# A decode block on one core: three edits around loads and the last softmax

## Chip, cores and metric

The kernel runs on one core of a Trainium2 chip. The metric is device microseconds (us) of one execution. All arithmetic is in 32-bit floats, and the core has a matrix engine (PE), a vector engine (DVE), a scalar engine (ACT), GpSimd (POOL) and a sync engine (SP). SP and ACT issue the transfers, which run on the core's 16 DMA engines.

## The reference

One token for each of four sequences goes through a layernorm, attention over the last 1024 positions of a cache (16 query heads, 8 key heads, head size 256), an output projection with a residual, and then an MLP with two layernorms before it.

```python
x = A_x                                            # (4, 1, 448)
h = x + attention(layernorm(x), k_cache, v_cache, wq, wo)
#   q = x @ wq; p = softmax(q k^T / 16) over the last 1024 keys; (p v) @ wo
h2 = h + mlp(layernorm(h))
#   y = layernorm(.); gelu(y @ w1 + b1) @ w2 + b2,  w1 (448, 1792), w2 (1792, 448)
```

## The kernel before, in words

All that is read from memory, about 88 MB, passes once through three large buffers ("slots", the tiles `t0`, `ta`, `tb`, `tc`, `td`, `te`). A slot of some 8 MB is filled by one or a few loads, used, and refilled when the products that read it are done. The host packs caches and weights so that each slot holds what a stage needs: `ta` has keys, query weights and the first half of the values of a head, `tb` the other half, output weights and the next keys, and so on.

SP issues all of these loads, in the order of the code: `wq0` with the transposed x (L262), `k0`, the keys of head 0 (L265), two small pieces of query weights `wq1_last` (L267), then `ta`, `tb`, `tc`, `td` twice (L290 to L311, all issued by the helper at L57), then the last slots `te`: keys of head 7, values and output weights of heads 6 and 7 (`vo`), `w1` in two loads and `w2` in three of 8, 4 and 2 chunks (L321 to L328). A chunk of w2 is 128 x 448 numbers. ACT issues four small transfers of 11 KB, the rows of x and of both biases (L127), into the tile `rs`, which is read only behind the attention.

Each transfer reports its end on one of eight counters, DMAHW0 to DMAHW7. The framework deals them in turn to the transfers in the order in which it schedules them, over SP's and ACT's queues together. A transfer that gets a counter for the second time first waits, on the engine that issues it, until the earlier user of that counter has landed. SP takes its instructions strictly in order, so what stands behind a waiting load waits too. In the kernel before, the order is `wq0` (0), `k0` (1), four rows (2 to 5), two `wq1_last` (6, 7), and then `ta` gets 0 again, `tb` 1, `tc` 2.

PE's order is that of the code. For a head it does the scores `s` (L174), DVE takes the maximum `mx` (L179), ACT the exponential `p` (L190), PE transposes it into `ppt` (L206), DVE copies that into `pT` (L210), and PE multiplies by the values into `po` (L218). Around the last softmax, where no other work is ready, the kernel issues products of a zero tile, `idle`, that nobody reads (L336): two between the scores of head 7 and the transposes, and ten between the transposes and the values of head 6 (L338 to L342). Then come head 6's output, head 7's values, the residual, the layernorms, and the MLP: `pu` from w1 (L416), `pa` from the first eight chunks of w2 (L449), `py` from the last six (L459), and the write of `out`.

Of the kernel before, what the change touches and what calls it, by code (L numbers as in the profile page):

```python
# [15 lines left out]
B, D = 4, 448  # L16
# [4 lines left out]
P = 128  # L21
# [3 lines left out]
NFC = F // P  # L25
FQ = F // 4
Q = 32
CACHE = NKC * B * DH
# [7 lines left out]
def block_kernel(ctx: ExitStack, tc, rows, wq0, k0, wq1, la, lb, lc, ld, k7, vo, w1, w2, out):  # L36
    nc = tc.nc
# [12 lines left out]
    def slot(name):  # L50
        return ring.tile([P, SLOT], F32, tag="r", name=name)

    def load(t, at, src, pieces=None):
        dst = t[:, at : at + src.shape[-1]]
        at = 0
        for n in pieces or (src.shape[-1],):
            nc.sync.dma_start(dst[:, at : at + n], src[:, at : at + n])  # L57
            at += n
        return dst

    def cut(t, sizes):
        parts, at = [], 0
        for n in sizes:
            parts.append(t[:, at : at + n])
            at += n
        return parts
# [11 lines left out]
    def keys(t):  # L78
        return t.rearrange("p (c b k) -> p c b k", c=2, b=B)
# [22 lines left out]
    yT = const.tile([P, ND + 1, Q], F32, name="yT")  # L102
# [21 lines left out]
    rs = const.tile([P, 2 * P + FQ], F32, name="rs")  # L124
    nc.gpsimd.memset(rs, 0.0)
    for j in range(4):
        nc.scalar.dma_start(rs[j * Q : j * Q + B, :], rows[j])  # L127
    xb, b2b, b1b = rs[:, :P], rs[:, P : 2 * P], rs[:, 2 * P :]


# [39 lines left out]
    def scores_half(g, h, kt):  # L170
        s = ps_s.tile([P, 512], F32, tag="s", name=f"s{g}_{h}")
        for c in range(2):
            for b in range(B):
                nc.tensor.matmul(  # L174
                    s[b * Q : (b + 1) * Q, :], qT[g % 2][:, c, b, :], kt[:, c, b, :],
                    start=(c == 0), stop=(c == 1),
                )
        m = work.tile([P, 1], F32, tag=f"mx{h}", name=f"mx{g}_{h}")
        nc.vector.reduce_max(m, s, axis=AX.X)  # L179
        return s, m  # L180

    def softmax(g, parts):
        halves, mx = zip(*parts)
        nm = work.tile([P, 1], F32, tag="nm", name=f"nm{g}")
        nc.vector.tensor_max(nm, mx[0], mx[1])
        nc.vector.tensor_scalar_mul(nm, nm, -SCALE)  # L186
        p = once.tile([P, 2 * 512], F32, tag="p", name=f"p{g}")
        sums = work.tile([P, 2], F32, tag="sums", name=f"sums{g}")
        for h in range(2):
            nc.scalar.activation(  # L190
                p[:, h * 512 : (h + 1) * 512], halves[h], AF.Exp, bias=nm, scale=SCALE,
                accum_out=sums[:, h : h + 1],
            )
        rec = work.tile([P, 1], F32, tag=f"rec{g % 3}", name=f"rec{g}")
        nc.vector.tensor_add(rec, sums[:, 0:1], sums[:, 1:2])
        nc.vector.reciprocal(rec, rec)
        return p, rec

    def scores(g, kt):
        return softmax(g, [scores_half(g, h, kt[h]) for h in range(2)])  # L200

    def transpose_p(g, p):
        for h in range(2):
            pt = ps_t.tile([P, 4, P], F32, tag="t", name=f"ppt{g}_{h}")
            for c in range(4):
                nc.tensor.transpose(pt[:, c, :], p[:, (4 * h + c) * P : (4 * h + c + 1) * P], ident)  # L206

            src = pt.rearrange("p (c i) (b q) -> p c i b q", i=2, b=B)
            for i in range(2):
                nc.vector.tensor_copy(  # L210
                    pT[g % 2][:, 2 * h : 2 * h + 2, :, i * REP : (i + 1) * REP], src[:, :, i, :, :REP]
                )
# [44 lines left out]
    def po_tile(g, pool=ps_o, tag="o"):  # L257
        return pool.tile([P, 2, DH], F32, tag=tag, name=f"po{g}")
# [22 lines left out]
    p, rec = scores(0, [keys(ka), keys(kb)])  # L281
# [7 lines left out]
    for g in (0, 3):  # L289
        ka, kb, wqt, va = cut(load(slot(f"ta{g}"), 0, la[g // 3]), (HALF, HALF, WEIGHTS, HALF))  # L290
        p, rec_next = scores(g + 1, [keys(ka), keys(kb)])
# [8 lines left out]
        p, rec_then = scores(g + 2, [keys(ka), keys(kb)])  # L300
# [11 lines left out]
        p, rec = softmax(g + 3, [first_half, scores_half(g + 3, 1, keys(kb))])  # L312
# [7 lines left out]
    g = HKV - 2  # L320
    e = [slot(f"te{i}") for i in range(3)]  # L321
    kt = [keys(t) for t in cut(load(e[0], 0, k7), (HALF, HALF))]
# [2 lines left out]
    vt_last = chunks(load(e[2], 0, vo[1][:, :CACHE], (CACHE // 4, CACHE // 2, CACHE // 4)))  # L325
    wo_last = output_weights(load(e[1], CACHE + WEIGHTS, vo[1][:, CACHE:]))
    w1t = cut(load(e[0], CACHE, w1, (2 * F, F + F // 2)), (F, F, F, F // 2))
    w2t = cut(load(e[2], CACHE, w2, (8 * D, 4 * D, 2 * D)), NFC * (D,))  # L328
    p, rec_last = scores(g + 1, kt)


    warm0 = ps_o.tile([P, 512], F32, tag="o", name="warm0")

    def keep_warm(n, warm):
        for _ in range(n):
            nc.tensor.matmul(warm[:Q], idle[:, :Q], idle, start=True, stop=True)  # L336

    keep_warm(2, warm0)  # L338
    transpose_p(g + 1, p)
    keep_warm(10, warm0)  # L340
    po = po_tile(g)
    values(g, vt, po)  # L342
    po_last = po_tile(g + 1, ps_t, "t")
# [17 lines left out]
    for i in range(4):  # L361
        for j in range(4):
            nc.tensor.matmul(
                ph[j * Q : (j + 1) * Q], oT[(g + 1) % 2][:, i, :], columns(wo_last[:, i, :], j),
                start=False, stop=(i == 3),
# [3 lines left out]
    def w1_part(a, j):  # L369
        if a < 3:  # L370
            return slice(0, P), w1t[a][:, FQ * j : FQ * (j + 1)]
        rows = slice(H * (j // 2), H * (j // 2) + H)
        return rows, w1t[a][rows, FQ * (j % 2) : FQ * (j % 2 + 1)]
# [38 lines left out]
    for a in range(ND):  # L412
        m = Q if a == 0 else B
        for j in range(4):
            rows, w = w1_part(a, j)
# [31 lines left out]
    for c in range(first):  # L447
        j, m = c % 4, Q if c < 4 else B
# [6 lines left out]
    for c in range(first, NFC):  # L455
        for j in range(4):
            m, n = (Q, 2) if c == first else (B, 2 if j < 3 else 1)
# [80 lines left out]
```

## Time and profile before

| | us |
|---|---|
| median of three runs | 215.27 |
| lowest and highest | 214.98, 215.72 |
| the profiled execution, its own time | 214.81 |
| its span, first to last instruction | 213.0 |

The profile is of one execution. Engine rows give busy time and what ended the idle time before it; "SPq" is SP's queue of issues; the chain of waits follows the last instruction back through whatever released each step.

### The profile page before, as it was taken

To read this page: it belongs to the slowest core of one execution; us is meant where nothing else is said; L and a number is where in the kernel's file an instruction comes from. 1 tells how busy PE (TensorE), PEld (TensorE's weight loads), DVE (VectorE), ACT (ScalarE), POOL (GpSimd) and SP (SyncE) were. 2 spreads that over 40 slices of the span, in tenths; PEclk is the share of its full clock that TensorE was granted. 3 is DMA by queue.
4 is the path that set the end of the run, shared out by engine and by line. 5 is a ranking of instruction groups with operands and counts; after the bars stand their busy time and mean duration, and the time that the engine had idled before them with its cause. 6 is when DMAs were issued, how large, how long until landed. Compare 5 with 4: busy or idle time off the path is not lost.

```text
span 213.0 us, 2294 instructions
## 1 busy us (share of the span) xinstructions
PE 137.4 (64%) x971; PEld 48.2 (23%) x971; DVE 38.4 (18%) x167; ACT 21.2 (10%) x52; POOL 5.6 (3%) x17
## 2 busy tenths in 40 slices
PE   0456824872970595289398198239809876998993
PEld 0322211220220221023123022113202322334432
DVE  1420320320230012012114013100301223122320
ACT  0210110120020100021003001000000302000310
POOL 6100000000000000000000000000000000000110
PEclk9999995796697579769859959955965999999999
DMA  7999899999999999999999999999999998999990
GB/s 291 433 392 502 381 486 391 447 467 409 417 453 444 417 417 477 390 465 391 458 423 444 425 456 417 429 417 465 405 410 415 430 450 380 435 414 435 420 376 34
DMA packets 3289, 88.46 MB, mean 415 GB/s; under 512 B 384, under 2 KB 512, under 8 KB 1104
## 3 DMA queue, kind: packets, MB, share of 16 engines
q1 hardware_dynamic: 3248, 88.29, 96.7%
q8 instruction: 7, 0.11, 0.2%
q10 hardware_dynamic: 32, 0.05, 0.1%
q14 instruction: 2, 0.02, 0.0%
HBM read 88.26 MB, written 0.07 MB: 415 GB/s over the span
## 4 chain that ended last, share of the span: by engine, by line
DMA 64%; PE 29%; DVE 3%; ACT 1%; issue 1%; SPq 0%; ACTq 0%; DVEq 0%
DMA ta<-la 21%; DMA td<-ld 20%; DMA tb<-lb 16%; PE s L174 8%; DMA t<-k 8%; PE po L218 8%; PE ppt L206 2%; PE pu L416 2%; PE warm L336 1%; PE acc L247 1%; PE pq L154 1%; PE pot L239 1%; PE pa L449 1%; DVE o L235 1%; DVE mx L179 1%
## 5 line engine op out<-in xcount | busy, mean ns | idle before, releaser
L179 DVE TENSOR_REDUCE mx<-s 128x1 f32<-128x512 f32 x16 | 11.1, 691 | 61.0 <-PE s L174 61.0
L174 PE MATMUL s<-ta,qT 128*32 128x512 f32 x64 | 12.2, 935 | 8.9 <-DMA ta<-la 8.9
L156 ACT COPY qs<-pq 128x512 f32<-128x512 f32 x8 | 4.7, 585 | 112.3 <-PE pq L154 112.3
L190 ACT ACTIVATE p<-s,nm 128x512 f32<-128x512 f32 x16 | 10.9, 687 | 45.9 <-DVE nm L186 45.9
L174 PE MATMUL s<-td,qT 128*32 128x512 f32 x32 | 7.3, 1061 | 12.0 <-DMA td<-ld 12.0
L235 DVE TENSOR_SCALAR o<-po,rec 128x512 f32<-128x512 f32 x8 | 6.0, 751 | 47.1 <-PE po L218 47.1
L218 PE MATMUL po<-tb,pT 128*32 128x512 f32 x32 | 7.3, 1061 | 10.4 <-DMA tb<-lb 10.4
L154 PE MATMUL pq<-tc,yT 128*32 128x512 f32 (+1 forms) x20 | 3.9, 890 | 14.8 <-DMA tc<-lc 14.8
L206 PE MATMUL ppt<-ident,p 128*128 128x128 f32 x64 | 10.5, 286 | 2.0 <-ACT p L190 1.7
L218 PE MATMUL po<-tc,pT 128*32 128x512 f32 x64 | 10.5, 815 | 0.0
L160 PE MATMUL pqt<-ident,qs 128*128 128x128 f32 x32 | 6.6, 341 | 6.0 <-ACT qs L156 6.0
L174 PE MATMUL s<-tb,qT 128*32 128x512 f32 x64 | 9.1, 717 | 0.0
L206 PEld LDWEIGHTS ppt<-ident,p 128*128 128x128 f32 x64 | 6.7, 140 | 7.1 <-ACT p L190 7.1
L218 PE MATMUL po<-te,pT 128*32 128x512 f32 x64 | 7.9, 596 | 0.1
L162 DVE TENSOR_REDUCE sm<-pqt 128x16 f32<-128x64 f32 x8 | 1.8, 224 | 33.9 <-PE pqt L160 33.9
L174 PE MATMUL s<-t,qT 128*32 128x512 f32 x32 | 6.1, 925 | 2.6 <-DMA t<-k 2.6
L218 PE MATMUL po<-td,pT 128*32 128x512 f32 x64 | 7.3, 595 | 0.0
L336 PE MATMUL warm<-idle 128*32 128x512 bf16 x25 | 7.3, 382 | 0.0
L160 PEld LDWEIGHTS pqt<-ident,qs 128*128 128x128 f32 x32 | 4.2, 169 | 12.1 <-ACT qs L156 10.3
L174 PEld LDWEIGHTS s<-ta,qT 128*32 128x32 f32 x64 | 2.9, 163 | 17.4 <-issue 14.4
L239 PE MATMUL pot<-ident,o 128*128 128x128 f32 x32 | 5.2, 287 | 2.2 <-DVE o L235 2.2
L148 POOL TENSOR_TENSOR r<-ve_r,mhalf 128x1 f32<-128x1 f32 x2 | 1.1, 542 | 192.2 <-DVE ve_r L147 192.2
(129 smaller groups left out, 113.4 us busy)
## 6 DMA issues: line engine op xcount, KB each, us to landing
tc<-lc SPq DMA_DIRECT2D x2, 7936.0 KB
td<-ld SPq DMA_DIRECT2D x2, 7936.0 KB
ta<-la SPq DMA_DIRECT2D x2, 7040.0 KB, 29.4
tb<-lb SPq DMA_DIRECT2D x2, 7040.0 KB, 34.3
te<-vo SPq DMA_DIRECT2D x1, 4992.0 KB, 27.2
t<-k SPq DMA_DIRECT2D x1, 4864.0 KB, 16.4
te<-k SPq DMA_DIRECT2D x1, 4096.0 KB, 36.9
te<-w SPq DMA_DIRECT2D x2, 1792.0 KB, 28.0
```

What stands on the lines that cost most here:

```text
L154: nc.tensor.matmul(pq[j * Q : (j + 1) * Q, cols], y, w, start=True, stop=True)
L156: nc.scalar.copy(qs, pq)
L160: nc.tensor.transpose(pt[:, i, :], qs[:, i * P : (i + 1) * P], ident)
L174: nc.tensor.matmul(s[b * Q : (b + 1) * Q, :], qT[g % 2][:, c, b, :], kt[:, c, b, :], start=(c == 0), stop=(c == 1),)
L179: nc.vector.reduce_max(m, s, axis=AX.X)
L190: nc.scalar.activation(p[:, h * 512 : (h + 1) * 512], halves[h], AF.Exp, bias=nm, scale=SCALE, accum_out=sums[:, h : h + 1],)
L206: nc.tensor.transpose(pt[:, c, :], p[:, (4 * h + c) * P : (4 * h + c + 1) * P], ident)
L218: nc.tensor.matmul(po[b * Q : (b + 1) * Q], pT[g % 2][:, c, b, :], vt[c][:, :, b, :], start=(c == 0), stop=(c == NKC // 2 - 1),)
L235: nc.vector.tensor_scalar_mul(o, po, rec)
L239: nc.tensor.transpose(pt[:, i, c], o[:, i, c * P : (c + 1) * P], ident)
L336: nc.tensor.matmul(warm[:Q], idle[:, :Q], idle, start=True, stop=True)
L416: nc.tensor.matmul(pu[j * Q : j * Q + m, :], zT[rows, a, :m], w, start=(a == 0), stop=(a == ND - 1),)
```

## The change

There are three edits.

The rows of x and the biases go in seven transfers instead of four: for three of the four quarters the columns of x and b2 (256) and those of b1 (448) are separate transfers. ACT issues them.

The loads of `w2` are cut into 8, 3, 2 and 1 chunks instead of 8, 4 and 2.

Around the last softmax a new helper, `fill`, multiplies a part of the keys of head 7, which have landed, by `yT`, in 32-bit floats, into the same tile that nobody reads. Two such products take the place of the two of `idle` ahead of the transposes; behind the transposes one such product and two of `idle` stand where ten of `idle` stood.

```diff
@@ rows of x and biases
     for j in range(4):
-        nc.scalar.dma_start(rs[j * Q : j * Q + B, :], rows[j])
+        parts = (slice(0, 2 * P), slice(2 * P, 2 * P + FQ)) if j < 3 else (slice(0, 2 * P + FQ),)
+        for cols in parts:
+            nc.scalar.dma_start(rs[j * Q : j * Q + B, cols], rows[j][:, cols])
@@ loads of the second MLP weights
-    w2t = cut(load(e[2], CACHE, w2, (8 * D, 4 * D, 2 * D)), NFC * (D,))
+    w2t = cut(load(e[2], CACHE, w2, (8 * D, 3 * D, 2 * D, D)), NFC * (D,))
@@ around the last softmax
+    def fill(n):
+        for _ in range(n):
+            nc.tensor.matmul(warm0[:Q], yT[:, 0, :], kt[0][:, 0, 0, :], start=True, stop=True)
+
+    fill(2)
+    transpose_p(g + 1, p)
+    fill(1)
     keep_warm(2, warm0)
-    transpose_p(g + 1, p)
-    keep_warm(10, warm0)
     po = po_tile(g)
```

The seven transfers use up eight counters sooner, and the dealing shifts by three. SP's queue at the start of the program stood like this (a row is line, operation, destination and source, size, and the counters it waits for):

```order
L57 DMA t_134<-wq 128x1808
L57 DMA t_134<-k 128x9728
L267 DMA wq_last<-wq 32x1x512 x2
L57 DMA ta_239<-la 128x14080 [waits DMAHW0_49]
L57 DMA tb_313<-lb 128x14080 [waits DMAHW1_49]
```

SP's queue at the same place stands now like this:

```order
L57 DMA t_137<-wq 128x1808
L57 DMA t_137<-k 128x9728
L269 DMA wq_last<-wq 32x1x512 [waits DMAHW1_49]
L269 DMA wq_last<-wq 32x1x512 [waits DMAHW2_49]
L57 DMA ta_242<-la 128x14080 [waits DMAHW3_49]
L57 DMA tb_316<-lb 128x14080 [waits DMAHW4_49]
```

The wait for counter 1, which is that of `k0`, has moved from `tb` up to the first `wq_last`, two places ahead of `ta`; `ta` and `tb` now wait for rows (counters 3 and 4).

At the program's end SP's queue held the second load of w1, the loads of w2 and the write of the output with these waits (counters 0, 1 and 2 are there those of the keys of head 7, of head 6's values and of the first quarter of head 7's values):

```order
L57 DMA te_813<-w 128x2688
L57 DMA te_815<-w 128x3584 [waits DMAHW0_49]
L57 DMA te_815<-w 128x1792 [waits DMAHW1_49]
L57 DMA te_815<-w 128x896 [waits DMAHW2_49]
L466 DMA out<-res 128x128 [waits DMAHW3_49,DVE_49]
```

Now SP's queue ends with these:

```order
L57 DMA te_818<-w 128x3584 [waits DMAHW3_49]
L57 DMA te_818<-w 128x1344 [waits DMAHW4_49]
L57 DMA te_818<-w 128x896 [waits DMAHW5_49]
L57 DMA te_818<-w 128x448 [waits DMAHW6_49]
L473 DMA out<-res 128x128 [waits DMAHW7_49,DVE_49]
```

The first three wait for the same three landings as before, by their new counters; the added last load waits for the middle half of head 7's values (counter 6), and the output for their last quarter.

On PE, between the scores of head 7 and the values of head 6, the rows after the change are these (`idle` is the zero tile; the second name behind the arrow is the weights' side):

```order
L176 MATMUL s_1_842<-te_816,qT_112 32x512 x8
L342 MATMUL warm_863<-te_816,yT 32x512 x2
L208 MATMUL ppt_0_866<-ident,p_856 128x128 x4
L208 MATMUL ppt_1_873<-ident,p_856 128x128 x4
L342 MATMUL warm_863<-te_816,yT 32x512
L338 LDWEIGHTS idle
L338 MATMUL warm_863<-idle 32x512
L338 LDWEIGHTS idle
L338 MATMUL warm_863<-idle 32x512
L220 MATMUL po_883<-te_817,pT_113 32x512 x16
```

Ahead of the transposes two products of `idle` have become two of the keys, and behind them ten of `idle` have become one of the keys and two of `idle`; everything else on PE keeps its place.

## The prediction, as put on record

> **What bounds the kernel now.** I read the page's slices first, then the chain of waits, then the stretches by DMA, then SP's queue, since the change touches loads. The head of the page, its DMA rows and the chain by engine:
>
> ```profile
> span 213.0 us, 2294 instructions
> ...
> DMA  7999899999999999999999999999999998999990
> GB/s 291 433 392 502 381 486 391 447 467 409 417 453 444 417 417 477 390 465 391 458 423 444 425 456 417 429 417 465 405 410 415 430 450 380 435 414 435 420 376 34
> ...
> DMA 64%; PE 29%; DVE 3%; ACT 1%; issue 1%; SPq 0%; ACTq 0%; DVEq 0%
> ```
>
> The DMA engines are 90% busy or nearly so in every slice but the first and the last, and 64% of the chain is waiting for loads. The chain's long pieces (start, length):
>
> ```profile
> 1.18 16.36 DMA t<-k
> ...
> 17.56 34.27 DMA tb<-lb
> ...
> 61.75 44.26 DMA ta<-la
> ...
> 117.86 42.28 DMA td<-ld
> ...
> 160.19 3.64 PE s L174 x16
> ```
>
> Behind 160.19 no piece of the chain is a load: from there PE, DVE and ACT lead to the end. So two things end close together, the stream of loads and the chain of arithmetic behind the landing of `td`. How full the stream is shows in a stretch from the first large load to the end (busy times, granted clock, DMA share, GB/s) and at its last two microseconds:
>
> ```profile
> 5.40:207.00 201.60, 134.62 (x907) 46.76 (x911) 37.32 (x161) 20.67 (x51) 2.11 (x3) 0.84 1.00 429
> ...
> 208.00:209.00 1.00, 0.77 (x29) 0.48 (x24) 0.00 (x0) 0.53 (x1) 0.00 (x0) 1.00 0.11 43
> 209.00:210.00 1.00, 0.99 (x39) 0.68 (x28) 0.00 (x0) 0.00 (x0) 0.00 (x0) 1.00 0.00 0
> ```
>
> A share of 1.00 over 201.6 us means that there is no hole in which a late load could catch up. Microseconds in which the DMA engines have nothing to do are added to the time. That decides which of the three edits matters.
>
> **Seven transfers of rows.** The bytes are the same. ACT issues three more, but has nothing else until the first copy of q; the tile is read behind the attention. What counts is the dealing of the counters, since it changes what SP waits for. SP's queue at the start, and what it waited for:
>
> ```profile
> 0.73 0.39 SPq L57 DMA_DIRECT2D t<-wq  x1
> 1.18 0.41 SPq L57 DMA_DIRECT2D t<-k  x1
> 1.63 1.55 SPq L267 DMA_DIRECT2D wq_last<-wq  x2
> 5.36 0.34 SPq L57 DMA_DIRECT2D ta<-la  x1
> 17.56 0.33 SPq L57 DMA_DIRECT2D tb<-lb  x1
> ```
>
> ```profile
> SPq L57 <- DMA t<-k: 11.9, 1, 11.9
> SPq L57 <- DMA t<-wq: 2.2, 1, 2.2
> ```
>
> Before, `ta` waits for counter 0 (`wq0`, landed at 5.36) and `tb` for counter 1: it goes out at 17.56, when `k0` has landed, 11.9 us after SP came to it. This wait was free, because `ta` had been queued behind `k0` for 12 us and filled the engines. By the order of SP's queue the wait for counter 1 now stands at the first `wq_last`. So `wq_last` (two), `ta`, `tb` and all behind them stay in SP until `k0` lands. Then nothing at all is queued.
>
> The hole, step by step. `k0` lands at 17.54 as before, since it runs ahead of `ta` either way. Both `wq_last` are then issued, 1.55 us by the row above, and `ta` goes out at 17.56 + 1.55 = 19.11. `tb` follows at once, as its rows have long landed. When `ta` lands is worked out from these rows (size, us from issue to landing):
>
> ```profile
> ta<-la SPq DMA_DIRECT2D x1, 7040.0 KB, 29.4
> ...
> t<-wq SPq DMA_DIRECT2D x1, 904.0 KB, 4.6
> ```
>
> Before, `ta` landed at 5.36 + 29.4 = 34.76, 17.22 us behind `k0`; with the two pieces of 64 KB between them that is 7168 KB in 17.22 us, 416 KB/us. At that rate `ta` alone takes 16.9 us. A load into an idle queue also has a start and an end that nothing covers. No row shows this for 7 MB. Nearest is `wq0`: 4.6 us less 904/416 = 2.2 gives 2.4. Smaller is the write of `out`, 64 KB (issue, and what waited for its landing):
>
> ```profile
> 210.39 0.35 SPq L466 DMA_DIRECT2D out<-res  x1
> ```
>
> ```profile
> SPq L532 <- DMA out<-res: 1.2, 1, 1.2
> ```
>
> 0.35 + 1.2 less 64/416 = 0.15 gives 1.4. So `ta` lands at 19.11 + 16.9 + 1.4 to 2.4, that is 37.4 to 38.4, or 2.7 to 3.7 us later than before. I take 3.4, nearer to `wq0`, which is a load and starts from idle. The ends are wider. If `k0`, alone in the queue, lands half a microsecond sooner, the low end is 2.2. If the 128 KB of `wq_last` must pass ahead of `ta`, another 0.3 makes the high end 4.0.
>
> The Trainium skill, DMA: Bandwidth & Descriptors, section Anatomy of one DMA, gives a fixed cost of about 2.0 us per transfer beside bytes over 436 GB/s, fitted on GpSimd's path, where these are SP's. It speaks against making one load wait for another's landing. By it the hole would be 3.3 us and the sum below 217.5; by `wq0` it is 3.7 and 217.9; by `out` 2.7 and 216.9. The rows stand in the sum.
>
> The late `wq_last` itself is covered. It is issued at 17.6 and 18.4 and, at 1.5 to 2.4 us from there, lands by 21; its product comes behind 32 records of scores:
>
> ```profile
> L154 PE MATMUL pq<-wq_last,yT x2: 589/601/613, 24.5 to 25.0; 64*32 64x512 f32 x2
> ```
>
> It is needed at 24.5, with over 3 us to spare.
>
> **The products around the softmax.** PE in the timeline (start, length; in brackets the idle time before):
>
> ```profile
> 174.62 3.62 PE L174 MATMUL s<-te,qT 128*32 128x512 f32 x32
> ...
> 180.32 1.32 PE L206 MATMUL ppt<-ident,p 128*128 128x128 f32 x8 [1.68 <-ACT p L190]
> ...
> 181.57 2.33 PE L336 MATMUL warm<-idle 128*32 128x512 bf16 x10
> 181.68 0.26 DVE L210 COPY pT<-ppt 128x16 f32<-128x16 f32 x2 [0.23 <-PE ppt L206]
> ...
> 183.97 4.50 PE L218 MATMUL po<-te,pT 128*32 128x512 f32 x40
> ```
>
> A product of `idle` costs 2.33/10 = 0.23 us. A product of the keys has the shape of the scores: 16 of them, 32 records, take 3.62 us. They go to four column groups in turn, so if the groups work side by side one alone takes 0.9 us, if not 0.23. I take 0.9, since the new ones all go to one group. Two in front take 1.8 us from about 178.2, to 180.0, and fit into the idle 1.68 us: the transposes wait for `p` until 180.32 as before. If each took 0.2 more, the transposes would start 0.1 late. Behind the transposes stand now 0.9 + 2 x 0.23 = 1.36 us instead of 2.33, so the values of head 6 start 0.95 us sooner, at 183.0 on the old scale. The last copy of `pT` is done at 181.94, and the values themselves:
>
> ```profile
> te<-vo SPq DMA_DIRECT2D x1, 4992.0 KB, 27.2
> ```
>
> ```profile
> 154.46 22.16 SPq L57 DMA_DIRECT2D te<-vo  x5
> ```
>
> They landed at 154.46 + 27.2 = 181.7, so there is room. With 0.23 the start would come 1.6 us sooner, but neither is worth its whole length, because the loads behind come next. The landings:
>
> ```profile
> 184.19 0.33 SPq L57 DMA_DIRECT2D te<-w  x1
> ```
>
> ```profile
> 201.95 1.80 PE L416 MATMUL pu<-te,zT 128*4 128x448 f32 x16
> ...
> 206.29 1.71 PE L449 MATMUL pa<-te,gT 128*32 128x448 f32 x16
> 207.83 0.35 PEld L459 LDWEIGHTS py<-te,gT 128*32 128x32 f32 x16 [0.65 <-DMA te<-w]
> ```
>
> The last w2 load went out at 184.19, when the first quarter of head 7's values had landed. The second w2 load, behind it by 2048 + 1024 + 896 + 1792 + 1344 + 1792 + 896 = 9792 KB, had landed by 207.83. That is 414 KB/us, so the second w1 load landed at 201.3, needed at 201.95, and the first w2 load at 205.7, needed at 206.29. Both have 0.6 us of slack. The stream and the chain of `td` shift together by the hole, so the arithmetic can gain 0.6 of the 0.95 before it meets w1 and w2. Gain: 0.6, between 0.2 and 0.95.
>
> **The loads of w2.** The wait for the second load ends at 207.83, but the copy of `pa` holds `py` up to 208.66 anyhow, so three chunks in place of four bring nothing. The added load holds nobody up: SP has only `out` behind it, and its counter, the middle half of head 7's values, lands some 5 us behind 184.19, when megabytes are still queued. Cost of both: 0, from -0.2 to +0.3, the price of one more short transfer at the stream's end.
>
> **Sum.** For the profiled execution: 214.81 + 3.4 - 0.6 + 0 = 217.6. Its own time lies 0.46 below the median of 215.27, so the forecast as a median is 218.1, or 1.3% slower.
>
> **Rivals.**
>
> *The hole is short* (18%). If the engines have `ta`'s first bytes moving right behind its issue, and `k0` lands sooner without a neighbour, the hole is 2.2 us or less, and with the gain of 0.6 the median is 216.9; with the full 0.95 it is 216.5. For it: the low `out` row. Against it: the 2.4 us of `wq0`.
>
> *The hole is long, or the tail gains nothing* (10%). With a hole of 4.0 us, fills that push the transposes by as much as they save behind them, and the 0.3 us of the short last load, the median is 214.81 + 4.0 + 0.3 + 0.46 = 219.6. The fills decide from about 1.3 us each: two then end 0.5 us too late, and the third with two of `idle` saves only that much. For it: PE ran at half rate behind the landing of `td`, 8 products of scores in 3.64 us, and the same landing comes now at another moment. Against it: the scores at 174.62 are at full rate again.
>
> *Faster: the hole is absorbed* (5%). Its place is the long middle. If a load there is issued late because its slot comes free late, the stream has slack of its own, and the products' 0.6 us are all that is left: 214.7. It decides from a slack of 3.4 us. Against it: a share of 1.00 over the whole stretch, and at each issue two earlier loads are still on their way, as the 34 to 44 us in the chain against 17 us for one load show.
>
> *It does not do what it says* (4%). If the wait at `wq_last` ended before `k0` landed, `ta` would go out at its old time, and the tail could still be held by w1 and w2 as before: 215.2. Against it: the same counter held `tb` until 17.56.
>
> **Chances and range.** The forecast holds 63%, from 217.3 to 219.1; the others 18, 10, 5 and 4. The range takes in both forms of the hole: low 216.4, high 219.7. It leaves out the two last cases and some of the third. A measurement of this kernel tells about 0.3%, 0.65 us, from no change. Faster by more: 0.05, within: 0.04, slower by more: 0.91.
>
> **What would show it.** In SP's queue, `wq_last` going out at 17.5 instead of 1.63 and `ta` near 19.1; in the stretches, a DMA share near zero between 18 and 20.5; `ta` landing near 38 and `td` near 163.5. On PE, one wait for `p` shortened to some tenths, and head 6's values starting 0.95 us sooner against the scores of head 7. In the tail, PE waiting for w1 or w2 for some tenths. I am wrong if `ta` still goes out near 5.4, if `td` lands no later, or if the transposes wait for the fills.

## The result, and the profile after

The changed kernel takes 218.87 us (median of six runs, 218.51 to 219.11), the kernel before beside it 215.5. The ratio is 1.0155, 95% interval 1.0131 to 1.0179: slower by 1.3 to 1.8%. The profiled execution took 218.80 us, 3.99 more than the one of before. Three single executions on record (the profiled ones of rows7_alone, 227.58 us, and of w2_alone, 248.46, and one of the kernel before, 228.48) were in a second, slower state, and everything below leaves them out.

The page of the kernel after begins so, with its DMA rows and the chain by engine:

```profile
span 217.0 us, 2293 instructions
...
DMA  7986899799989989999989999998999999999991
GB/s 285 453 355 194 384 446 488 343 491 414 480 386 410 506 386 410 476 395 457 460 374 478 409 480 389 421 492 386 410 453 399 436 427 416 424 402 437 425 382 49
...
DMA 76%; PE 17%; SPq 2%; DVE 1%; ACT 1%; issue 1%; DVEq 0%; ACTq 0%
```

The fourth slice, 16.3 to 21.7 us, has 194 GB/s where before had 502. No other slice has fallen like it. The chain has moved too: waiting for loads is 76% of it, and one piece is a load in the tail. SP's queue of the kernel after, from the start, and what it waited for there:

```profile
0.73 0.39 SPq L57 DMA_DIRECT2D t<-wq  x1
1.18 0.41 SPq L57 DMA_DIRECT2D t<-k  x1
17.34 1.55 SPq L269 DMA_DIRECT2D wq_last<-wq  x2
18.94 0.44 SPq L57 DMA_DIRECT2D ta<-la  x1
19.42 0.43 SPq L57 DMA_DIRECT2D tb<-lb  x1
```

```profile
SPq L269 <- DMA t<-k: 15.7, 1, 15.7
```

The two `wq_last` went out at 1.63 before and go out at 17.34 now, the moment `k0` has landed; `ta` follows at 18.94 instead of 5.36. The stretch around it, in the kernel after and then in the kernel before (DMA share and GB/s are the last two numbers):

```profile
15.00:20.50 5.50, 3.25 (x17) 0.90 (x20) 0.48 (x3) 0.00 (x0) 0.00 (x0) 1.00 0.55 176
```

```profile
15.00:20.50 5.50, 2.93 (x17) 0.91 (x20) 0.48 (x3) 0.00 (x0) 0.00 (x0) 1.00 0.98 417
```

Within these 5.5 us, 241 GB/s less, 1.33 MB, is 3.1 us of the stream at its 429 GB/s. By single microseconds the kernel after shows where the engines ran dry:

```profile
16.00:17.00 1.00, 0.00 (x0) 0.00 (x0) 0.00 (x0) 0.00 (x0) 0.00 (x0) 1.00 0.11 30
17.00:18.00 1.00, 0.54 (x4) 0.23 (x8) 0.00 (x0) 0.00 (x0) 0.00 (x0) 1.00 0.00 0
18.00:19.00 1.00, 1.00 (x8) 0.22 (x4) 0.00 (x0) 0.00 (x0) 0.00 (x0) 1.00 0.07 12
19.00:20.00 1.00, 1.00 (x9) 0.23 (x5) 0.00 (x0) 0.00 (x0) 0.00 (x0) 1.00 0.28 80
```

From 16 to 20 the share lies between 0.00 and 0.28. So the engines had almost nothing to do from more than 1 us before SP saw the landing of `k0` (17.34) until 1 us after the issue of `ta` (18.94). Shares of such short stretches are rough: the next microsecond has 2.55. PE's first products on each load, in the kernel after, show where the shift went (start, length, line and operation; in brackets PE's wait for the landing):

```profile
38.65 5.67 PE L176 MATMUL s<-ta,qT 128*32 128x512 f32 x32 [10.66 <-DMA ta<-la]
55.93 3.64 PE L220 MATMUL po<-tb,pT 128*32 128x512 f32 x16 [6.11 <-DMA tb<-lb]
74.91 1.93 PE L156 MATMUL pq<-tc,yT 128*32 128x512 f32 x10 [8.28 <-DMA tc<-lc]
93.66 3.64 PE L176 MATMUL s<-td,qT 128*32 128x512 f32 x16 [5.10 <-DMA td<-ld]
...
126.94 3.64 PE L220 MATMUL po<-tb,pT 128*32 128x512 f32 x16 [5.81 <-DMA tb<-lb]
146.26 1.94 PE L156 MATMUL pq<-tc,yT 128*32 128x512 f32 x10 [8.28 <-DMA tc<-lc]
165.01 3.64 PE L176 MATMUL s<-td,qT 128*32 128x512 f32 x16 [6.64 <-DMA td<-ld]
206.11 1.80 PE L423 MATMUL pu<-te,zT 128*4 128x448 f32 x16 [0.41 <-DMA te<-w]
```

Before, the first four began at 34.90, 51.88, 70.66 and 89.41, the next three at 122.69, 141.44 and 160.19. So each landing is later, by 3.75, 4.05, 4.25, 4.25, 4.25, 4.82 and 4.82 us: nothing is ever caught up. The last row is new: PE now waits for the second load of w1. Around the softmax, PE of the kernel after:

```profile
182.31 1.88 PE L342 MATMUL warm<-te,yT 128*32 128x512 f32 x4
...
184.59 1.32 PE L208 MATMUL ppt<-ident,p 128*128 128x128 f32 x8 [0.40 <-ACT p L192]
...
185.84 1.04 PE L342 MATMUL warm<-te,yT 128*32 128x512 f32 x2
...
186.72 0.59 PE L338 MATMUL warm<-idle 128*32 128x512 bf16 x2
...
187.37 4.50 PE L220 MATMUL po<-te,pT 128*32 128x512 f32 x40
```

The idle time ahead of the transposes is 0.40 us, where it was 1.68, and the values of head 6 start 3.40 us later than before, with `td` 4.82 later. The write of `out` goes out at 214.61, 4.22 later. So 1.42 of the 4.82 had been won back by the values, and 0.82 of that is given back, nearly all of it in waits for the last loads: 0.37 for values of head 7 and 0.41 for the second load of w1.

### The profile page after: what moved, and what is told of

It reads as the page before. It is cut to its first block, busy times and chain, and to the rows that moved or that the text cites. A ratio compares the mean times of both kernels' runs of the same rounds, so it can differ in the third digit from the quotient of the medians.

```text
span 217.0 us, 2293 instructions
## 1 busy us (share of the span) xinstructions
PE 135.0 (62%) x967; PEld 47.7 (22%) x967; DVE 38.4 (18%) x167; ACT 21.2 (10%) x52; POOL 5.6 (3%) x17
## 4 chain that ended last, share of the span: by engine, by line
DMA 76%; PE 17%; SPq 2%; DVE 1%; ACT 1%; issue 1%; DVEq 0%; ACTq 0%
DMA ta<-la 21%; DMA td<-ld 20%; DMA tb<-lb 17%; DMA te<-w 11%; DMA t<-k 7%; PE s L176 6%; PE po L220 4%; SPq L57 1%; PE ppt L208 1%; PE pq L156 1%; PE acc L249 1%; PE pu L423 1%; PE pa L456 1%; SPq L269 1%; PE pqt L162 1%
## 5 line engine op out<-in xcount | busy, mean ns | idle before, releaser
L176 PE MATMUL s<-ta,qT 128*32 128x512 f32 x64 | 11.0, 850 | 13.4 <-DMA ta<-la 13.4
L176 PE MATMUL s<-tb,qT 128*32 128x512 f32 x64 | 8.1, 647 | 0.0
L212 DVE COPY pT<-ppt 128x16 f32<-128x16 f32 x32 | 4.7, 171 | 7.6 <-PE ppt L208 7.6
```

The costliest lines, as they stand in the source:

```text
L176: nc.tensor.matmul(s[b * Q : (b + 1) * Q, :], qT[g % 2][:, c, b, :], kt[:, c, b, :], start=(c == 0), stop=(c == 1),)
L212: nc.vector.tensor_copy(pT[g % 2][:, 2 * h : 2 * h + 2, :, i * REP : (i + 1) * REP], src[:, :, i, :, :REP])
```

## The experiments

Twelve kernels ran, in three groups, each group beside runs of the kernel before (medians 215.33, 215.16 and 214.97). The theory: the rows shift the counters, the wait for `k0` now stands ahead of `ta`, and the hole passes whole to the end; the products win back what the landings of w1 and w2 allow. The rivals: small transfers cost by themselves; the rows cost nothing; it is the kind of product, or the cut of w2, that gains.

**rows7_alone.** The kernel before with the seven transfers of rows.

```diff
-        nc.scalar.dma_start(rs[j * Q : j * Q + B, :], rows[j])
+        parts = (slice(0, 2 * P), slice(2 * P, 2 * P + FQ)) if j < 3 else (slice(0, 2 * P + FQ),)
+        for cols in parts:
+            nc.scalar.dma_start(rs[j * Q : j * Q + B, cols], rows[j][:, cols])
```

> The kernel before, with only the seven transfers of rows. Theory (the dealing of counters puts the wait for k0 ahead of ta, and the hole in the stream passes to the end): ta goes out near 18.9 instead of 5.4, td lands 4.2 to 4.8 us later, and the median is 219.5 to 220.3, more than the changed kernel's 218.9, since the gain of the products is missing. Rival (the products gain nothing, the whole loss of 3.4 us is the rows'): 218.9. Rival (the rows cost nothing): 215.5.

Measured: 219.27 us, ratio 1.0185 (1.0153 to 1.0218), that is 4.0 us more than before, between 3.3 and 4.7. The rows carry the whole loss. Whether they carry more than it, the interval does not tell: it holds 218.9 too.

**tail_alone.** The changed kernel with the rows in four.

```diff
-        parts = (slice(0, 2 * P), slice(2 * P, 2 * P + FQ)) if j < 3 else (slice(0, 2 * P + FQ),)
-        for cols in parts:
-            nc.scalar.dma_start(rs[j * Q : j * Q + B, cols], rows[j][:, cols])
+        nc.scalar.dma_start(rs[j * Q : j * Q + B, :], rows[j])
```

> The changed kernel with the rows in four transfers again, so only the products and the cut of w2. Theory: the values of head 6 start 0.95 us sooner, of which 0.6 remains when w1 and w2 are met: 214.9. Rival (all of it remains): 214.5. Rival (the products delay the transposes or the cut of w2 costs something): 215.5 or more.

Measured: 214.28 us, ratio 0.9948 (0.993 to 0.9966). Without the rows the change is a gain of 0.7 to 1.5 us, more than the 0.6 expected. Its ten runs lie between 214.16 and 214.47, where the 15 runs of before beside them lie between 214.68 and 216.2. That narrowness had not been expected and is taken up below. Its trace shows what holds it, the second load of w1 on PE:

```profile
201.34 1.80 PE L421 MATMUL pu<-te,zT 128*4 128x448 f32 x16 [0.43 <-DMA te<-w]
```

**rows5_alone.** Before, with five transfers of rows: counter 1 falls to `ta` itself.

```diff
-        nc.scalar.dma_start(rs[j * Q : j * Q + B, :], rows[j])
+        parts = (slice(0, 2 * P), slice(2 * P, 2 * P + FQ)) if j < 1 else (slice(0, 2 * P + FQ),)
+        for cols in parts:
+            nc.scalar.dma_start(rs[j * Q : j * Q + B, cols], rows[j][:, cols])
...
-            m, n = (Q, 2) if c == first else (B, 2 if j < 3 else 1)
+            m, n = (Q, 2) if c == first else (B, 2 if j < 1 else 1)
```

The second change stands in the last products, `py`, and is no part of the question. It makes this kernel leave out products that the second and third quarter of the output need, so it does not compute the block; it serves for its times alone. They are hardly touched: from the start of the last `py` to the write of `out` are 1.44 us, 1.45 before.

> The kernel before with five transfers of rows. The counters then fall so that ta itself waits for k0, and both wq_last go out early. Theory (what costs is where the wait for k0 stands): ta goes out at 17.4 to 17.6, the hole is shorter by the two wq_last issues of 1.55 us, and the median is 217.8 to 218.4. Rival (what costs is the number of small transfers, about 1.2 us for each added one): 216.7.

Measured: 218.65 us, ratio 1.0153 (1.0125 to 1.018). SP's queue and the landing of `ta`:

```profile
1.63 4.45 SPq L269 DMA_DIRECT2D wq_last<-wq  x2
17.72 0.34 SPq L57 DMA_DIRECT2D ta<-la  x1
```

```profile
37.40 5.23 PE L176 MATMUL s<-ta,qT 128*32 128x512 f32 x32 [8.58 <-DMA ta<-la]
```

One added transfer costs 3.3 us, so the number of transfers is not what costs. The median is 0.25 us above the theory's 217.8 to 218.4. The two issues no longer lie in the hole, and it is smaller by 1.2 us at `ta`, but the second `td` lands 3.53 late, since 0.4 and later 0.6 come in on the way. In the profiled execution `out` is written 4.16 late, and the 0.6 beyond the 3.53 is PE's clock, which is taken up with idle6.

**rows8_alone.** Before, with eight transfers of rows: counter 1 falls to the eighth row, on ACT.

```diff
-        nc.scalar.dma_start(rs[j * Q : j * Q + B, :], rows[j])
+        parts = (slice(0, 2 * P), slice(2 * P, 2 * P + FQ)) if j < 4 else (slice(0, 2 * P + FQ),)
+        for cols in parts:
+            nc.scalar.dma_start(rs[j * Q : j * Q + B, cols], rows[j][:, cols])
...
-            m, n = (Q, 2) if c == first else (B, 2 if j < 3 else 1)
+            m, n = (Q, 2) if c == first else (B, 2 if j < 4 else 1)
```

Here too `py` is changed along with it: the fourth quarter's products cover their columns twice, which changes nothing in the output.

> The kernel before with eight transfers of rows. Now the eighth row, on ACT's queue, gets the counter of k0, and SP waits only for rows. Theory: ta goes out near 8 us, ACT stands still until 17.4, so that the first scores come some 4 us later, under ta's and tb's loads; the median is within 0.5 of before, 215.0 to 216.0. Rival (the number of small transfers costs): 219.5 or more. Rival (ACT's standstill passes to the end): 219.5 too, but with ta early and the stream without a hole.

Measured: 217.68 us, ratio 1.0103 (1.0068 to 1.0137). The expectation failed in one step. SP did wait for rows alone, but these landed far later than supposed. SP's queue and its waits in this kernel:

```profile
10.65 0.82 SPq L269 DMA_DIRECT2D wq_last<-wq  x1
```

```profile
13.81 0.68 SPq L269 DMA_DIRECT2D wq_last<-wq  x1
```

```profile
17.04 0.34 SPq L57 DMA_DIRECT2D ta<-la  x1
```

```profile
SPq L269 <- DMA rs<-rows: 11.4, 2, 9.1
SPq L57 <- DMA rs<-rows: 2.5, 1, 2.5
```

SP saw the first three rows land at 10.65, 13.81 and 17.04, though ACT had begun to issue at 4.07. So `ta` still had a hole in front of it, and PE's first products on it come 1.77 us late:

```profile
36.67 3.64 PE L176 MATMUL s<-ta,qT 128*32 128x512 f32 x16 [6.37 <-DMA ta<-la]
```

ACT stood still until 17.5 and the first scores came at 21.24 instead of 17.68, yet `ta` found PE waiting 6.37 us for it. So that standstill was covered, as expected, and the loss of the stream follows the issue of `ta` here too. In the profiled execution `out` is written 3.45 late with `td` only 2.49 late; the rest is again PE's clock.

The four kernels whose profiles are read, by the issue of `ta`, in us:

| | `ta` issued | PE starts on `ta` | from issue | PE starts on the second `td` | median |
|---|---|---|---|---|---|
| before | 5.36 | 34.90 | covered by `k0` | 160.19 | 215.33 |
| rows8_alone | 17.04 | 36.67 | 19.63 | 162.68 | 217.68 |
| rows5_alone | 17.72 | 37.40 | 19.68 | 163.72 | 218.65 |
| after | 18.94 | 38.65 | 19.71 | 165.01 | 218.87 |

The median of before is that beside rows8_alone and rows5_alone; beside the kernel after it was 215.5. From issue to use `ta` takes 19.6 to 19.7 us in each of the other three. Of these, 16.9 are its bytes at 416 KB/us; 2.7 to 2.8 are start and end that nothing covers.

**rows7_pool.** All three edits, with the three added rows on GpSimd's queue.

```diff
-        for cols in parts:
-            nc.scalar.dma_start(rs[j * Q : j * Q + B, cols], rows[j][:, cols])
+        for i, cols in enumerate(parts):
+            (nc.gpsimd if i else nc.scalar).dma_start(rs[j * Q : j * Q + B, cols], rows[j][:, cols])
```

> The changed kernel, all three edits, but the three added transfers of rows are issued by GpSimd, whose transfers are counted apart, so that SP's first waits are those of before. Theory (only the place of the wait for k0 costs): ta goes out near 5.4, td lands at 160.2, and the median is that of the products and the w2 cut without the rows, 214.1 to 214.6. Rival (seven small transfers cost by themselves, on whatever queue): 217 or more.

Measured: 214.57 us, ratio 0.9967 (0.995 to 0.9983). SP's queue of this kernel:

```profile
1.63 1.55 SPq L269 DMA_DIRECT2D wq_last<-wq  x2
5.34 0.34 SPq L57 DMA_DIRECT2D ta<-la  x1
```

The same seven transfers, dealt other counters, and 4.3 us have gone. As three of them also went by another queue, it takes the other two kernels to settle it: on ACT's queue one added transfer cost 3.3 us and four cost 2.3, so neither the transfers nor their queue cost, but the place of the wait.

**fills_alone, w2_alone, idle6.** Which part of the tail gains. The first is the kernel before with only the new products, the second with only the cut of w2, the third with six products of `idle` behind the transposes.

```diff
 # fills_alone
+    fill(2)
+    transpose_p(g + 1, p)
+    fill(1)
     keep_warm(2, warm0)
-    transpose_p(g + 1, p)
-    keep_warm(10, warm0)
 # w2_alone
-    ... w2, (8 * D, 4 * D, 2 * D)
+    ... w2, (8 * D, 3 * D, 2 * D, D)
 # idle6
-    keep_warm(10, warm0)
+    keep_warm(6, warm0)
```

> The kernel before with only the new products around the softmax. Theory (all of the tail's gain is theirs): 214.2 to 214.5. Rival (the cut of w2 gives a part of it): 214.6 to 215.0.

> The kernel before with only the loads of w2 cut into 8, 3, 2 and 1. Theory (the copy of pa holds the last products anyhow): 215.3, within 0.3. Rival (py comes earlier): down to 214.9. Rival (one more short transfer at the stream's end): up to 215.7.

> The kernel before with six products of idle behind the last transposes instead of ten, nothing else: 1.36 us instead of 2.27, the same length as the new block. Theory (the gain is the shorter block): 214.2 to 214.7. Rival (products on landed keys in the idle time ahead of the transposes are what gains): 215.3, no change.

Measured: fills_alone 214.46 (ratio 0.9966, 0.9949 to 0.9983), w2_alone 214.87 (0.9991, 0.997 to 1.0011), idle6 214.6 (0.9972, 0.9955 to 0.999). The cut of w2 is worth nothing that can be measured; the products carry the tail's gain; and a shorter block of `idle` gains about as much as products on keys. But the profile of idle6 shows something else. PE around its softmax, and the stretches there (the third number from the end is the granted clock):

```profile
179.49 1.34 PE L206 MATMUL ppt<-ident,p 128*128 128x128 f32 x8 [1.68 <-ACT p L190]
180.76 2.74 PE L336 MATMUL warm<-idle 128*32 128x512 bf16 x6
```

```profile
178.00:180.00 2.00, 0.51 (x4) 0.42 (x4) 0.48 (x3) 1.34 (x4) 0.00 (x0) 1.00 1.03 440
180.00:182.00 2.00, 1.99 (x9) 0.84 (x8) 0.69 (x6) 0.11 (x2) 0.00 (x0) 0.67 0.80 336
182.00:184.00 2.00, 1.94 (x8) 0.50 (x10) 0.00 (x0) 0.00 (x0) 0.00 (x0) 0.50 1.11 467
```

Behind the 1.68 us without a product the clock fell to 0.50, and six products took 2.74 us, where ten took 2.33 before. In before's first profile, with the same gap, it did not fall. The profiles of rows5_alone and rows8_alone have the same gap too, and there it did fall; their ten products took so long:

```profile
184.16 3.93 PE L338 MATMUL warm<-idle 128*32 128x512 bf16 x10
```

```profile
183.36 4.02 PE L338 MATMUL warm<-idle 128*32 128x512 bf16 x10
```

From the scores of head 7 to the values of head 6 these two executions took 1.6 and 1.7 us longer than before's first profile; 1.0 and 0.7 of that they had gained ahead of it, as the clock had come back sooner behind `td`.

That gave a new question: is part of what the products on keys gain a steady clock?

**front_fill, no_front.** Two kernels for that. In front_fill only the two products ahead of the transposes are on keys and the ten behind stay; in no_front there are none ahead.

```diff
 # front_fill
-    keep_warm(2, warm0)
+    fill(2)
     transpose_p(g + 1, p)
     keep_warm(10, warm0)
 # no_front
-    keep_warm(2, warm0)
     transpose_p(g + 1, p)
```

> The kernel before with only the two products of idle ahead of the transposes replaced by two of the keys; the ten behind stay. Before's profile has 1.68 us of idle PE there, and in the run with six products of idle the granted clock fell to 0.50 behind that same gap. Theory (part of the gain is that the gap no longer lets the clock fall): no clock below 0.9 between 180 and 190, the runs lie within 0.5 of each other, median 214.6 to 215.0. Rival (only the shorter block behind gains): 215.2, and the spread of before, 214.4 to 216.4.

> The kernel before without the two products of idle ahead of the last softmax's transposes, so PE has some 2.3 us without a product there instead of 1.68. Theory (the gap lets the clock fall): clock 0.50 for some 3.4 us behind the transposes in more of the runs, and the median 215.6 to 216.6. Rival (the length of the gap does not matter, PE waits for p anyhow): 215.2.

Measured: front_fill 214.73 us, ratio 0.9977 (0.9962 to 0.9992), its 12 runs from 214.41 to 215.06; no_front 215.54, ratio 1.0016 (0.9998 to 1.0034), from 214.75 to 216.03. So with the long block behind unchanged, filling the gap ahead gains about 0.5 us and takes away more than half of the spread (0.65 us, beside 1.63 of before in the same group; 0.5 was expected). Leaving it emptier points the other way, but the interval still touches no change, and the median stays just under the 215.6 that the theory asked for. Both fit a clock that falls behind the gap in some executions. That it falls was seen in three profiles, those of idle6, rows5_alone and rows8_alone. The profiles of front_fill and no_front have 1.00 throughout the softmax, and no_front's, at 214.76, is one of its fastest.

The traces show when it falls. PE's clock is at 0.50 when `td` lands and comes back some us later, at another moment in each execution. In the three profiles with a fall, the fall comes 17.1 us after that return, and the clock stays low for 3.4 us, a fifth of 17.1. The whole gap lies within the 3.4 us ahead of the fall. In both profiles of before and in no_front's, steps of 3.4 us counted from the return cut the gap in two, and the clock does not fall. In tail_alone, rows7_pool and the kernel after the gap would lie whole within a step, but the products on keys fill it, and the clock stays at 1.00: tail_alone's came back at 163.56, idle6's at 163.60, and only idle6's fell. So the filling prevents the fall, as far as nine profiles can tell. What sets the moment of the return was not found.

**before_again.** The kernel before, profiled once more.

> The kernel before once more, for another profile. Theory (its spread of 2 us comes from PE's clock behind gaps, while the stream is the same): td lands at 160.2 within 0.2 as in the first profile, and if the run is above 215.5 the clock is at 0.50 for some us between 180 and 190; if it is below 214.9 it is not. Rival (the spread is the stream's): td's landing moves with the time.

Measured: 214.8 us; the second `td` is used from 160.18, and the clock is 1.00 from 178 to 192. It is the low end of the spread, like the first profile, so the upper end of before's spread (up to 216.4) has no profile here. The stream was in the same place to 0.01 us.

**finer_loads.** tail_alone with the loads of w1 and w2 cut finer, to take away the wait that holds it.

```diff
-    w1t = cut(load(e[0], CACHE, w1, (2 * F, F + F // 2)), (F, F, F, F // 2))
-    w2t = cut(load(e[2], CACHE, w2, (8 * D, 3 * D, 2 * D, D)), NFC * (D,))
+    w1t = cut(load(e[0], CACHE, w1, (2 * F, F, F // 2)), (F, F, F, F // 2))
+    w2t = cut(load(e[2], CACHE, w2, (4 * D, 4 * D, 3 * D, 2 * D, D)), NFC * (D,))
```

> The new products and rows in four transfers, with w1 in loads of 2, 1 and 1/2 parts instead of 2 and 1 1/2, and w2 in 4, 4, 3, 2 and 1 chunks. Theory (the tail is held by the landing of the second w1 load, 0.4 us of waiting): its wait goes, the first w2 load lands sooner too, and the median falls by 0.2 to 0.4 to 213.9 to 214.2. Rival (smaller loads cost at the stream's end as much): 214.3 or more.

Measured: 214.17 us, ratio 0.9959 (0.9946 to 0.9972). That overlaps tail_alone's. Its wait list, for PE in the tail:

```profile
PE py L464 <- DMA te<-w: 0.6, 1, 0.6
```

The wait for w1 has gone from PE's products, and one for w2 has taken its place: the stream's end itself holds the tail now. tail_alone and finer_loads are the fastest versions found, faster than both kernels.

## Why the prediction was right

**The wait's place**, forecast: `wq_last` at 17.5, `ta` at 19.11. Seen: 17.34 and 18.94, with SP waiting 15.7 us for `k0`. rows5_alone, rows8_alone and rows7_pool show that it is the place of the wait that costs: the loss follows the issue of `ta`, not the number of transfers, and is gone when SP's waits are those of before.

**Where the hole lies**: off. The share near zero was forecast between 18 and 20.5 and was seen from 16 to 20, so most of it lies ahead of `ta`'s issue: the engines had run dry before SP saw `k0` land.

**The hole passes whole to the end**: right. Every landing in the trace is later by as much as the one ahead of it, or by more.

**The size of the hole** was the term that was too small: 3.4 us forecast (2.2 to 4.0), 3.75 measured at `ta` and 4.82 at the second `td`. The cost of a load into an empty queue was put at some 2.1, between `out`'s 1.4 and `wq0`'s 2.4; three issues of `ta` give 2.7 to 2.8. Even `wq0`, the nearer row, was low. The rest came later, where the prediction had no term at all. From `ta` to `tb` the landings lie 16.98 us apart before and 17.28 after, 17.38 in rows5_alone and 17.67 in rows8_alone. From the second `tb` to `tc` they lie 18.75 apart before and in rows8_alone, and 19.32 and 19.35 after and in rows5_alone. The first of these is partly scatter, for nine profiles without the hole have 16.98 to 17.21 from `ta` to `tb`. The second is not: all nine have 18.74 to 18.76 there. What makes it was not found.

**The products.** Their length, 0.9 us each, was right (1.88 us for two), and so was it that the transposes wait for `p` as before. The cap was right too: PE waits for the second w1 load, 0.41 us, and the net gain in the profile is 4.82 - 4.22 = 0.60, the 0.6 of the sum. The landing of w1 sets this figure, whatever is won ahead of it, and what was won is made of other parts than the sum had. The stretch from `td` to the scores of head 7 was 0.56 us shorter in this execution (13.87 us instead of 14.43), since PE's clock came back sooner: query products took 1.20 us of the chain instead of 1.77. With the products' 0.86 that is 1.42, of which the last loads took back 0.82.

**In medians** the products gain more than 0.6, from 0.4 to 1.1 us in fills_alone, as the kernel before has a spread of 2 us that they remove; the forecast set out from one profiled execution at the low end of it. The two errors have opposite signs: rows +4.0 instead of +3.4, products -0.7 instead of -0.6, together +3.3 against a measured +3.3 (0.0155 x 215.5). With tail_alone's -1.1 the sum would be +2.9; the intervals allow both, so that the first comes out even is partly luck.

**The cut of w2**, forecast 0: 0.9991 with 1 inside the interval. Right, for the kernel before. Beside the products it was not measured by itself: fills_alone, without the cut, has PE wait 0.38 us for w2, where tail_alone has no such wait.

**The late `wq_last`** cost nothing, as forecast: its first product, at 24.52 before, comes at 24.26.

**The rivals.** A short hole is excluded by the landings, absorption by all of them, and no effect by SP's queue. The long hole came nearest to the truth: 4.8 us at `td`, but with the tail's gain kept.

## What to carry to other kernels

A kernel that is held by its stream of loads pays for each moment in which no load is queued, and pays it whole at the end, so look at what each load waits for before it is issued, and not only at what it moves. Where completion counters are dealt in turn, one more small transfer on any queue that shares them can move a wait from a harmless place to the head of the stream: compare the waits in the issue order of both programs, not the code. Shorten the arithmetic behind the last loads only as far as the landings allow; beyond that the next landing is the bound.

## What the runs showed of the hardware

Small transfers of 4 and 7 KB, issued on ACT's queue from 4.07 us while the 4864 KB of `k0` were moving, were seen by SP to land at 10.65, 13.81 and 17.04 in rows8_alone: one about every 3.2 us, and the first 6.6 us after ACT began to issue.

The DMA engines' share was between 0.00 and 0.28 from 16 to 20 in the kernel after, while `k0`'s landing reached SP at 17.34 and `ta` was issued at 18.94. A wait for a landing ahead of the next load thus left them idle on both sides of it.

A 7040 KB load issued into an empty queue took 19.6 to 19.7 us until PE used it, three times within 0.1 us, 2.7 to 2.8 more than its bytes at the rate of the full stream.

PE's granted clock can fall to 0.50 behind a gap of 1.68 us in one execution and stay at 1.00 behind the same gap in another. It fell in idle6, rows5_alone and rows8_alone, each time 17.1 us after it had come back and for 3.4 us, and stayed at 1.00 in both profiles of before.
